# Block 0's second product: half of it by seven block products, and one load of k moved behind the turns of x

## The chip, the cores and the metric

One core of one Trainium2 chip. The metric is device time in microseconds (us) of one execution. Engines: TensorE (PE, with its weight loads PEld), VectorE (DVE), ScalarE (ACT), GpSimd (POOL) and SyncE (SP), which here only issues DMAs.

## The reference

Batch 8, 8 heads, 576 positions, head dimension 64. A linear attention with cosine and sine features is followed by a two-layer network whose activation is a quick gelu:

```python
def phi(x, c, s):
    r = np.maximum(x, 0.0)
    return np.concatenate([r * c, r * s], axis=-1)
q_p, k_p = phi(q, cos_w, sin_w), phi(k, cos_w, sin_w)
kv = np.einsum('bhsf,bhsd->bhfd', k_p, v)
z = np.sum(k_p, axis=2)
num = np.einsum('bhsf,bhfd->bhsd', q_p, kv)
den = np.einsum('bhsf,bhf->bhs', q_p, z)[..., None] + 1e-06
x = num / den                  # to (4608, 512)
h = x @ w_in                   # (4608, 2048)
g = h * (1.0 / (1.0 + np.exp(-1.702 * h)))
return g @ w_out               # (4608, 512)
```

## The kernel before

A block is the first 512 tokens of one batch; the last 64 tokens of each batch are gathered into one tail that is worked at the end. All matmuls take bf16 and accumulate in fp32. The order of the instructions on every engine is the order in which the code emits them (a manual schedule), so each engine is a queue that stops at its first unmet wait.

For each batch, VectorE or ScalarE makes the features of k (`trig`, line 161: two instructions, cosine and sine, for each of nine slices) and of q (`trig_q`, line 176, two for each of five chunks), and v is cast (`vcopy`, line 187). SP turns q's features with DMA transposes (`qturn_dma`, 217). A key/value product of 72 matmuls (`kv_next`, 794, line 237) is evacuated by VectorE (line 245). `num_mm` (304) makes numerator and denominator of one chunk of 128 tokens, `num_div` (315) divides on VectorE in three instructions (lines 321, 323, 325), and the chunk is turned into x's layout, by TensorE and ScalarE (`xturn_mm`, `xturn_evac`) for batch 1 or by a DMA on SP (`xturn_dma`, 351) from batch 2 on.

The first product (x by w_in) fills accumulators of the PSUM pool `pmm`, which has four banks taken in turn; ScalarE writes the gelu of each to g. The second product (g by w_out) has 16 steps of 128 (`fc`). In the blocks from 1 on it is done by seven block products instead of eight (`wino_mm`, 509): g and w_out are cut in two along the inner dimension, g along its tokens and w_out along its columns, VectorE makes four sums of blocks of g (`g_sums`, 466) and four of blocks of w_out (`w_sum_1`, `w_sums`, 441 to 451, made once), and seven products p1, p2, p6, p5, p7, p3, p4 go to three banks w, y and x. Between the products a bank is copied by ScalarE (`keep`, 528) or added to a kept copy by VectorE (`join`, 539). Batches 2 to 6 do the same to part of the first product in pairs of units (`mm1_pair`, 724, class `Unit`).

Block 0 is different: its second product is plain. `mm2` (416) makes, for each of four groups of 128 tokens, 16 matmuls 512 columns wide, and ScalarE writes the bank to the result tile `ty` (line 427). These 64 matmuls stand between the tail of the first product (`mm1_tail_first`) and `start_block(1)` (798), which begins block 1's first product: four accumulators, chunk by chunk, while x's chunks 2 and 3 are divided and turned. In between stand the key/value product of batch 1 and the chunks 0 to 2 of its x. On VectorE the features of k of batch 1, the sums of w_out and three of the five chunks of q stand beside it.

The loads of the batches go through SP's queue: q, k and v of batch 2 after batch 1's turns of q (lines 935, 936). In block 1, at `fc` 6, the features of batch 2's k are made, and then k and q of batch 3 are loaded, k first:

```python
if nb is not None and fc == f0 + 1:
    kv_operands(nb)
    if nb + 1 < B:
        load(kf, k, nb + 1, nc.sync)
        load_q(nb + 1, nc.sync)
```

Then come block 1's seven products, between which batch 2's x is made and turned by SP (`x_next`), v of batch 3 is loaded after the fourth turn, and ScalarE makes the features of batch 3's q. `mm1_pair` for batch 2 begins with the sums of x (line 635 on) and the features of batch 3's k on VectorE, among which the additions of the paired units stand (line 667).

Of the kernel before, what the change touches and what calls it, by code (L numbers as in the profile page):

```python
# [9 lines left out]
F32 = mybir.dt.float32  # L10
BF16 = mybir.dt.bfloat16
AF = mybir.ActivationFunctionType
MUL = mybir.AluOpType.mult
ADD = mybir.AluOpType.add
MAX = mybir.AluOpType.max
SUB = mybir.AluOpType.subtract
# [4 lines left out]
def kernel(  # L21
# [9 lines left out]
    nc = tc.nc  # L31
    B, H, S, D = q.shape
    d_model = H * D
    d_ff = moe_w_in.shape[1]
    KC = d_model // 128
    FC = d_ff // 128
    NS = S // 64
# [7 lines left out]
    ypool = ctx.enter_context(tc.tile_pool(name="ypool", bufs=4))  # L45
    small = ctx.enter_context(tc.tile_pool(name="small", bufs=3))
    pmm = ctx.enter_context(tc.tile_pool(name="pmm", bufs=4, space=PSUM))
# [76 lines left out]
    def load(t, src, b, eng=nc.gpsimd):  # L124
        eng.dma_start(out=t, in_=src_of(src, b))
# [50 lines left out]
    def trig_q(c, act=False):  # L176
        n = 128 if c < 4 else 64
        i = chunk(qf, c)
        for cs, w in enumerate((cosw, sinw)):
            o = qn[0:n, c, :, ts(cs, 64)]  # L180
            sc = w[0:n, NS + c:NS + c + 1]
            if act:
                nc.scalar.activation(o, i, AF.Relu, scale=sc)  # L183
            else:
                nc.vector.tensor_scalar(o, i, 0.0, sc, op0=MAX, op1=MUL)
# [31 lines left out]
    def qturn_dma(c):  # L217
        n = 128 if c < 4 else 64
        nc.sync.dma_start_transpose(out=qT[:, :, c * 128:c * 128 + n],
                                    in_=qn[0:n, c].rearrange("p h f -> p (h f)"))  # L220
# [108 lines left out]
    x = {}  # L329
# [43 lines left out]
    def mm1(b, fc):  # L373
        mm1_part(b, fc, 0, MT)
        gelu(fc)
# [9 lines left out]
    def mm1_tail_first(half):  # L385
        hps = pmm.tile([128, 8, 64], F32, name="mm")
        for f in range(8):
            for kc in range(KC):
                nc.tensor.matmul(hps[:, f], wcol(kc, half * 8 + f), xt[:, kc, 0:64],
                                 start=(kc == 0), stop=(kc == KC - 1))  # L390
        nc.scalar.activation(gt0[:, ts(half, 8)], hps, AF.Gelu_apprx_sigmoid)
# [7 lines left out]
                             hps[:, 64:B * 64].rearrange("p (b a t) -> p b a t", a=2, t=32),  # L399
                             AF.Gelu_apprx_sigmoid)  # L400

    yp = {}

    later = []
    out_j = out[0:S].rearrange("(p j) d -> j p d", j=NS)
# [1 line left out]
    def rows(b, t):  # L407

        if t == 4:
            return [(64 * u, 64, out_j[NS - 1] if b + u == 1 else out[(b + u) * S - 64:(b + u) * S])  # L410
                    for u in range(2)]
        if b == 0:
            return [(64 * u, 64, out_j[2 * t + u]) for u in range(2)]
        return [(0, 128, out[b * S:b * S + 512].rearrange("(p c) d -> c p d", c=4)[t])]

    def mm2(b, t, lo, hi, c0=0, c1=d_model):
        if lo == 0:
            yp[b, t, c0] = pmm.tile([128, d_model], F32, name="mm")
        for fc in range(lo, hi):
            w = gT[fc // 4][:, fc % 4, ts(t, 128)] if t < 4 else gt[:, fc, ts(b // 2, 128)]  # L420
            nc.tensor.matmul(yp[b, t, c0][:, c0:c1], w, w_out_sb[:, fc, c0:c1],  # L421
                             start=(fc == 0), stop=(fc == FC - 1))
        if hi == FC:
            if t % 2 == 0:
                st["y0"] = ypool.tile([128, 2, d_model], F32, name=f"ty{t // 2}", bufs=1)
            ysb = st["y0"][:, t % 2]
            nc.scalar.activation(ysb[:, c0:c1], yp[b, t, c0][:, c0:c1], AF.Identity)
            for p0, n, dst in rows(b, t):
                later.append((dst[:, c0:c1], ysb[p0:p0 + n, c0:c1]))

    HF = FC // 2
# [4 lines left out]
    sg = {n: sums[:, i].rearrange("p (f t) -> p f t", f=HF)  # L438
          for i, n in enumerate(("s1", "s2", "s3", "s4"))}

    def w_sum_1():
        nc.vector.tensor_tensor(wt["t1"], wq[0, 1], wq[0, 0], op=SUB)

    def w_sums(h):

        tt = nc.vector.tensor_tensor
        o = {n: wt[n][:, ts(h, 4)] for n in wt}
        w = {n: wq[n][:, ts(h, 4)] for n in wq}
        tt(o["t2"], w[1, 1], o["t1"], op=SUB)
        tt(o["t3"], w[1, 1], w[0, 1], op=SUB)  # L450
        tt(o["nt4"], w[1, 0], o["t2"], op=SUB)
# [256 lines left out]
    def pair_slot():  # L708
        pair_no[0] += 1
        return pair_slots[pair_no[0] % 7].rearrange("p (f t) -> p f t", f=2)  # L710

    def x_pair(b):
        t = xpool.tile([128, KC, MT], BF16, name="xT")
        xp[b] = {n: t[:, i].rearrange("p (k t) -> p k t", k=2) for i, n in enumerate(("t1", "t2", "t3", "nt4"))}
        for n in xp[b]:
            x_sum(b, n, xp[b])
# [81 lines left out]
    def start_block(b):  # L798

        for c in range(4):  # L800
            for fc in range(4):
                mm1_part(b, fc, c * 128, c * 128 + 128)
            if c == 0:
                num_mm(3)
                num_div(3)
                xturn_mm(2)
                xturn_evac(b, 2)
            if c == 1:
                num_mm(4)
                num_div(4)  # L810
                xturn_mm(3)
                xturn_evac(b, 3)
        for fc in range(4):
            gelu(fc)
        mm1(b, 4)
        xturn_dma(b, 4)
# [101 lines left out]
    load_wout(3)  # L918
    for n in ws_pair:
        win_sum(n, 0, ws_pair)  # L920
    for j in range(NS):
        trig(kr, kf, j)
    w_sum_1()
    for fc in range(8, FC):
        mm1(0, fc)
    mm1_tail_first(0)
    mm1_tail_first(1)
    for c in range(5):
        trig_q(c, act=(c > 2))
        qturn_dma(c)  # L930
    w_sums(0)
    vcopy(0, 2)
    vcopy(2, 4, act=True)
    w_sums(1)
    load_q(2, nc.sync)
    load_kv(2)
    for g in range(2):
        for t in range(4):
            mm2(0, t, 4 * g, 4 * g + 4)
    for t in range(4):  # L940
        mm2(0, t, 8, 12)
    kv_next()
    mm2(0, 0, 12, 16)
    x_open(1)
    num_mm(0)
    num_div(0)
    mm2(0, 1, 12, 14)
    num_mm(1)
    num_div(1)
    mm2(0, 1, 14, 16)  # L950
    xturn_mm(0)
    xturn_evac(1, 0)
    mm2(0, 2, 12, 16)
    xturn_mm(1)
    xturn_evac(1, 1)
    num_mm(2)
    num_div(2)
    mm2(0, 3, 12, 16)
    start_block(1)

    def kv_operands(b):
        for j in range(NS):
# [4 lines left out]
    def x_next(b, c):  # L967
        num_mm(c)
        num_div(c)
        xturn_dma(b, c)  # L970


    for b in range(1, B):
        nb = b + 1 if b + 1 < B else None
        if nb is None:
            break
        f0 = 5 if b == 1 else 0
        if b in PAIR:
            mm1_pair(b, nb)
        for fc in range(f0, FC) if b not in PAIR else ():  # L980
            if b == 1 and fc == f0:
                for c in range(5):
                    trig_q(c)
                    qturn_dma(c)
            if nb is not None and fc == f0 + 1:
                kv_operands(nb)

                if nb + 1 < B:
                    load(kf, k, nb + 1, nc.sync)
                    load_q(nb + 1, nc.sync)  # L990
            if fc == 8 and b == 1:
                vcopy()
            if fc == 12:
                g_sums(("s1", "s2"), 0)
            mm1(b, fc)
        if nb is not None:
            x_open(nb)
            if b == 1:
                kv_mm_next()
            g_sums(("s1", "s2"), 1)  # L1000
            if b == 1:
                kv_evac(0, 4)
                g_sums(("s3",), 0)
            at = ({2: [0], 3: [1], 4: [2], 6: [3], 8: [4]} if b == 1 else
                  {s: [p if nb < B - 1 else (0, 4, 1, 2, 3)[p]] for p, s in enumerate((0, 1, 3, 4, 6))})
            wino_open()
            for p in range(7):
                for c in range(2):
                    wino_mm(p, c)
                    s = 2 * p + c  # L1010
                    if c == 1:
                        wino_after(b, p)
                    for c2 in at.get(s, ()):
                        x_next(nb, c2)
                        if c2 == 3 and nb + 1 < B:
                            load(vf, v, nb + 1, nc.sync)

                    s0 = 4 if b > 2 else 8
                    if s0 <= s < s0 + 5 and nb + 1 < B:
                        trig_q(s - s0, act=True)  # L1020
                    if 8 <= s < 13 and nb + 1 < B:
                        qturn_dma(s - 8)
                    if s == 4 and b > 1:
                        for n in ("s3", "s4"):
                            g_sums((n,), 0)
                            g_sums((n,), 1)
                    if s == 2 and b == 1:
                        g_sums(("s3",), 1)
                    if s == 4 and b == 1:
                        g_sums(("s4",), 0)  # L1030
                    if s == 6 and b == 1:
                        g_sums(("s4",), 1)
            if nb in PAIR:
                x_pair(nb)
# [107 lines left out]
```

## Time and profile before

| what | value |
|---|---|
| median of three runs | 274.7 us (274.24 to 275.27) |
| the profiled execution | 274.66 us, its span 272.9 us |
| granted TensorE clock | 0.998 |
| 64 matmuls of block 0's second product, line 421 | 33.42 to 50.30, with other work between |
| key/value product of batch 1 / of batch 2 | starts at 43.88 / 65.49 |
| first matmul of block 1, line 365 | 50.13 |
| first paired block (batch 2) | from 80.13 |

The profile gives start, duration, engine, line, operation and tiles of each instruction, in us from the span's start. A bracket at the end of a row tells how long the engine was idle before it and what ended that. Instructions of one engine overlap: the next starts somewhat before the one before it has ended, so the distance of starts, not the duration, is the price of one in a series. A matmul's end is modelled, too. A DMA has its issue on its queue and a landing, which is a mark on a semaphore from each of 16 engines.

### The profile page before, as it was taken

How to read it: one execution, taken by the hardware profiler on the slowest of the kernel's cores; microseconds unless marked ns; L12 is line 12 of the kernel's file. 1: busy time of each engine (PE TensorE's matmuls, PEld its weight loads, DVE VectorE, ACT ScalarE, POOL GpSimd, SP SyncE). 2: the span in 40 equal slices, each digit the busy share in tenths (PEclk: the TensorE clock that was granted, in tenths of full speed). 3: DMA queues.
4: the chain of work that ended last, by engine and by line, in shares of the span. 5: the costliest groups of instructions: out<-in, count | busy, mean ns of one | idle time of the engine just before them, and what ended most of it. 6: DMA issues, size and time to landing. Idle time of an engine off the chain costs nothing.

```text
span 272.9 us, 7034 instructions
## 1 busy us (share of the span) xinstructions
PE 264.9 (97%) x2844; PEld 206.3 (76%) x2864; DVE 207.8 (76%) x487; ACT 174.7 (64%) x316; POOL 39.8 (15%) x66
## 2 busy tenths in 40 slices
PE   8899999999999999999999999999999999999995
PEld 2585645856986788778877887788778876999984
DVE  4947766689869799779988898789888995744741
ACT  6967632585289728983888487858684147677621
POOL 5691000000121012101110022001300173000010
PEclk9999999999999999999999999999999999999999
DMA  7999999999999979999999699999990654000343
GB/s 240 252 211 299 270 297 144 252 325 173 337 228 309 243 202 175 194 209 320 235 280 250 193 142 260 171 286 208 231 214 4 108 154 137 0 2 0 78 116 115
DMA packets 74031, 53.66 MB, mean 197 GB/s; under 512 B 53024, under 2 KB 63776, under 8 KB 74000
## 3 DMA queue, kind: packets, MB, share of 16 engines
q1 hardware_dynamic: 68032, 37.37, 61.6%
q0 software_dynamic: 5968, 15.86, 23.9%
q8 instruction: 22, 0.36, 0.6%
q14 instruction: 9, 0.07, 0.1%
HBM read 36.70 MB, written 9.44 MB: 169 GB/s over the span
## 4 chain that ended last, share of the span: by engine, by line
PE 88%; DVE 4%; ACT 3%; DMA 2%; issue 1%; SPq 0%; ACTq 0%
PE mm L520 28%; PE mm L658 15%; PE mm L365 13%; PE at L721 9%; PE mm L421 5%; PE at L520 4%; PE mm L396 4%; PE at L237 4%; PE at L310 3%; DMA kf<-in_k_dram 2%; ACT qn L183 2%; DVE xn L325 1%; DVE kr L169 1%; PE at L342 1%; PE mm L205 1%
## 5 line engine op out<-in xcount | busy, mean ns | idle before, releaser
L520 PEld LDWEIGHTS <-sums 128*128 128x128 bf16 x448 | 41.8, 98 | 6.0 <-DVE sums L477 1.1
L526 POOL DMA_DIRECT2D out_dram<-ysb x24 | 17.4, 725 | 180.5 <-DVE den L321 101.1
L520 PE MATMUL mm<-wsum,sums 128*128 128x256 bf16 x336 | 40.6, 273 | 0.0
L365 PE MATMUL mm<-xT,w_in 128*128 128x512 bf16 (+1 forms) x240 | 37.8, 304 | 1.1 <-issue 0.9
L520 PEld LDWEIGHTS <-g 128*128 128x128 bf16 x336 | 32.0, 98 | 4.6
L371 ACT ACTIVATE g<-mm 128x512 bf16<-128x512 f32 x42 | 24.1, 598 | 9.9 <-PE mm L365 9.9
L365 PEld LDWEIGHTS <-w_in 128*128 128x128 bf16 x248 | 21.3, 114 | 11.7
L721 PE MATMUL at<-xT,w_in 128*128 128x512 bf16 x110 | 27.8, 379 | 0.5
L325 DVE TENSOR_TENSOR xn<-at,inv 128x512 bf16<-128x512 f32 x39 | 27.0, 691 | 1.3
L520 PE MATMUL mm<-w_out_sb,g 128*128 128x256 bf16 x224 | 27.4, 273 | 0.0
L169 DVE TENSOR_SCALAR kr<-kf,cosw 128x256 bf16<-128x256 f32 x69 | 24.5, 355 | 3.6 <-DMA kf<-in_k_dram 3.6
L169 DVE TENSOR_SCALAR kr<-kf,sinw 128x256 bf16<-128x256 f32 x68 | 23.6, 348 | 0.0
L658 PE MATMUL mm<-xT,w_in 128*128 128x256 bf16 x152 | 22.0, 273 | 0.0
L658 PE MATMUL mm<-xT,gt 128*128 128x256 bf16 x160 | 21.6, 272 | 0.4 <-ACT gt L672 0.4
L183 ACT ACTIVATE qn<-qf,cosw 128x512 bf16<-128x512 f32 (+1 forms) x27 | 19.2, 711 | 3.6 <-DMA qf<-in_q_dram 2.6
L658 PEld LDWEIGHTS <-w_in 128*128 128x128 bf16 x168 | 18.6, 113 | 3.3
L658 PEld LDWEIGHTS <-gt 128*128 128x128 bf16 x160 | 17.6, 113 | 2.8 <-issue 0.5
L721 PEld LDWEIGHTS <-w_in 128*128 128x128 bf16 x120 | 13.5, 113 | 8.2
L183 ACT ACTIVATE qn<-qf,sinw 128x512 bf16<-128x512 f32 (+1 forms) x27 | 19.1, 708 | 0.0
L371 ACT ACTIVATE g<-at 128x512 bf16<-128x512 f32 x30 | 17.5, 597 | 2.0 <-PE at L721 1.3
L535 ACT ACTIVATE kept_p<-mm 128x512 f32<-128x512 f32 (+1 forms) x15 | 8.5, 565 | 16.0 <-PE mm L520 14.2
L535 ACT ACTIVATE kept_u<-mm 128x512 f32<-128x512 f32 (+1 forms) x8 | 4.3, 544 | 18.9 <-PE mm L520 18.9
(175 smaller groups left out, 467.7 us busy)
## 6 DMA issues: line engine op xcount, KB each, us to landing
kf<-in_k_dram SPq DMA_DIRECT2D x6, 1152.0 KB, 9.6
vf<-in_v_dram SPq DMA_DIRECT2D x6, 1152.0 KB, 6.6
qf<-in_q_dram SPq DMA_DIRECT2D x6, 1024.0 KB, 6.0
out_dram<-ysb POOLq DMA_DIRECT2D x24, 256.0 KB, 5.5
w_out_sb<-in_moe_w_out_dram POOLq DMA_DIRECT2D x4, 512.0 KB, 17.6
kf<-in_k_dram POOLq DMA_DIRECT2D x1, 1152.0 KB, 13.2
vf<-in_v_dram POOLq DMA_DIRECT2D x1, 1152.0 KB, 21.0
w_in<-in_moe_w_in_dram POOLq DMA_DIRECT2D x2, 512.0 KB, 10.1
```

What stands on the lines that cost most here:

```text
L169: eng.tensor_scalar(o, i, 0.0, w[:, j:j + 1], op0=MAX, op1=MUL)
L183: nc.scalar.activation(o, i, AF.Relu, scale=sc)
L237: nc.tensor.matmul(st["kv", i][:, hh, ds(col, n)], kr[r, j, i, :], rhs(r, i, j), start=(j == 0), stop=(j == NS - 1))
L325: nc.vector.tensor_tensor(xn, pv[:, :, :, 0:64], inv.unsqueeze(3).to_broadcast([128, 2, 4, 64]), op=MUL)
L365: nc.tensor.matmul(hp[fc][:, t0:t1], wcol(kc, fc), x[b][:, kc, t0:t1], start=(kc == 0), stop=(kc == KC - 1))
L371: nc.scalar.activation(gT[fc // 4][:, fc % 4], hp.pop(fc), AF.Gelu_apprx_sigmoid)
L421: nc.tensor.matmul(yp[b, t, c0][:, c0:c1], w, w_out_sb[:, fc, c0:c1], start=(fc == 0), stop=(fc == FC - 1))
L520: nc.tensor.matmul(bank[to][c], lhs, rhs, start=opens, stop=(fc == HF - 1), skip_group_check=True)
L526: eng.dma_start(out=dst[:, 2 * i + c0:2 * i + c1, ts(n, HD)], in_=t[:, c0:c1])
L535: nc.scalar.activation(o, i, AF.Identity)
L658: nc.tensor.matmul(to[:, j], lhs, rhs, start=(opens and j == 0 and k == 0), stop=(k == 1), skip_group_check=True)
L721: nc.tensor.matmul(hp[fc], wcol(kc, fc), x[b][:, kc], start=(kc == 0), stop=(kc == KC - 1))
```

## The change

Two things are changed. The inner steps 0 to 7 of block 0's second product are done by seven block products on half-size blocks, with an extra bank z; the steps 8 to 15 are then added by plain matmuls 256 wide into the four banks. The sums of g's blocks go to the tile `sums`, those of w_out there too (the t1 sum stays in `wsum`); two of k's nine slices go from VectorE to ScalarE, the last two chunks of q's features are emitted after the copy of p5, and the second half of the sums of w_out for later blocks is emitted after `start_block(1)`. Three of the four results are written by VectorE (with the kept copy added), one by ScalarE; they go to DRAM where they did before. And the load of k of batch 3 is emitted after the fourth turn of batch 2's x, ahead of the load of v.

```diff
-    def w_sum_1():
-        nc.vector.tensor_tensor(wt["t1"], wq[0, 1], wq[0, 0], op=SUB)
+    def w_sum_1(h):
+        nc.vector.tensor_tensor(wt["t1"][:, ts(h, 4)], wq[0, 1][:, ts(h, 4)], wq[0, 0][:, ts(h, 4)], op=SUB)
...
+    def g_sums_0():
+        tt = nc.vector.tensor_tensor
+        o = sums0
+        tt(o["s1"], g0(1, 0), g0(1, 1), op=ADD)
+        tt(o["s2"], o["s1"], g0(0, 0), op=SUB)
+        tt(o["s3"], g0(0, 0), g0(1, 0), op=SUB)
+        tt(o["s4"], g0(0, 1), o["s2"], op=SUB)
+
+    def w_sums_0():
+        tt = nc.vector.tensor_tensor
+        o = sums0
+        w_sum_1(0)
+        tt(o["t2"], w0(1, 1), o["t1"], op=SUB)
+        tt(o["t3"], w0(1, 1), w0(0, 1), op=SUB)
+        tt(o["nt4"], w0(1, 0), o["t2"], op=SUB)
+
+    def open_0():
+        for n in ("x", "w", "y", "z"):
+            t = pmm.tile([128, 2, HD], F32, name="mm")
+            bank[n] = [t[:, c] for c in range(2)]
+            bank[n, "all"] = t
+
+    def prod_0(p):
+        name, to, a, w = PRODUCTS[p]
+        for c in range(2):
+            for f in range(4):
+                lhs = sums0[a][:, f, ts(c, 128)] if isinstance(a, str) else g0(a[1], a[2])[:, f, ts(c, 128)]
+                rhs = sums0[w][:, f] if isinstance(w, str) else w0(*w)[:, f]
+                nc.tensor.matmul(bank[to][c], lhs, rhs, start=(name in OPENS and c == 0 and f == 0),
+                                 stop=(name in OPENS and f == 3), skip_group_check=True)
+
+    def plain_0(to, i, n, lo, hi, cs=range(2)):
+        for c in cs:
+            for fc in range(lo, hi):
+                nc.tensor.matmul(bank[to][c], gT[fc // 4][:, fc % 4, ts(2 * i + c, 128)], wq[1, n][:, fc - HF],
+                                 start=(to == "z" and c == 0 and fc == HF), stop=(fc == FC - 1), skip_group_check=True)
...
+    def out_0(to, i, n, with_=None):
+        o = y0[i][:, :, ts(n, HD)]
+        if with_ is None:
+            nc.scalar.activation(o, bank[to, "all"], AF.Identity)
+        else:
+            nc.vector.tensor_tensor(o, bank[to, "all"], with_, op=ADD)
...
-    for j in range(NS):
+    g_sums_0()
+    for j in range(NS - 2):
         trig(kr, kf, j)
-    w_sum_1()
+    w_sums_0()
+    w_sum_1(1)
     for fc in range(8, FC):
         mm1(0, fc)
+    trig(kr, kf, NS - 2, act=True)
     mm1_tail_first(0)
+    trig(kr, kf, NS - 1, act=True)
     mm1_tail_first(1)
-    for c in range(5):
-        trig_q(c, act=(c > 2))
+    open_0()
+    prod_0(0)
+    keep("p1", "x")
+    prod_0(1)
+    prod_0(2)
+    for c in range(3):
+        trig_q(c)
         qturn_dma(c)
+    keep("u2", "x")
+    prod_0(3)
+    keep("p5", "y")
+    for c in (3, 4):
+        trig_q(c, act=True)
+        qturn_dma(c)
+    prod_0(4)
+    nc.vector.tensor_tensor(kept0, bank["x", "all"], kept["p5"], op=ADD)
     w_sums(0)
     vcopy(0, 2)
     vcopy(2, 4, act=True)
-    w_sums(1)
     load_q(2, nc.sync)
     load_kv(2)
-    for g in range(2):
-        for t in range(4):
-            mm2(0, t, 4 * g, 4 * g + 4)
-    for t in range(4):
-        mm2(0, t, 8, 12)
+    prod_0(5)
+    prod_0(6)
+    for to, i, n in (("w", 0, 0), ("y", 0, 1), ("x", 1, 0), ("z", 1, 1)):
+        plain_0(to, i, n, 8, 12)
     kv_next()
-    mm2(0, 0, 12, 16)
+    plain_0("x", 1, 0, 12, 16)
+    out_0("x", 1, 0)
     x_open(1)
     num_mm(0)
     num_div(0)
-    mm2(0, 1, 12, 14)
+    plain_0("w", 0, 0, 12, 16, (0,))
     num_mm(1)
     num_div(1)
-    mm2(0, 1, 14, 16)
+    plain_0("w", 0, 0, 12, 16, (1,))
+    out_0("w", 0, 0, kept["p1"])
     xturn_mm(0)
     xturn_evac(1, 0)
-    mm2(0, 2, 12, 16)
+    plain_0("y", 0, 1, 12, 16)
     xturn_mm(1)
     xturn_evac(1, 1)
     num_mm(2)
     num_div(2)
-    mm2(0, 3, 12, 16)
+    out_0("y", 0, 1, kept["u2"])
+    plain_0("z", 1, 1, 12, 16)
+    out_0("z", 1, 1, kept0)
...
     start_block(1)
+    w_sums(1)
...
-                    load(kf, k, nb + 1, nc.sync)
                     load_q(nb + 1, nc.sync)
...
                             x_next(nb, c2)
+                        if c2 == 3 and b == 1:
+                            load(kf, k, nb + 1, nc.sync)
                         if c2 == 3 and nb + 1 < B:
                             load(vf, v, nb + 1, nc.sync)
```

More of the change, by code (lines that the diff above doesn't have):

```diff
@@ L400, in mm1_tails @@
                              AF.Gelu_apprx_sigmoid)
-    yp = {}
     later = []
@@ L414, in rows @@
         return [(0, 128, out[b * S:b * S + 512].rearrange("(p c) d -> c p d", c=4)[t])]
[L416 to L429, printed above, removed]
     HF = FC // 2
@@ L710, in pair_slot, with g0, w0 @@
         return pair_slots[pair_no[0] % 7].rearrange("p (f t) -> p f t", f=2)
+    sums_flat = sums.rearrange("p n e -> p (n e)")
+    sums0 = {n: sums_flat[:, ts(i, 1024)].rearrange("p (f t) -> p f t", f=4)
+             for i, n in enumerate(("s1", "s2", "s3", "s4", "t2", "t3", "nt4"))}
+    sums0["t1"] = wt["t1"][:, 0:4]
+    kept0 = pair_slots[0].rearrange("p (c d) -> p c d", c=2)
+    def g0(i, k):
+        return gT[k][:, :, ts(i, 256)]
+    def w0(k, n):
+        return wq[0, n][:, ts(k, 4)]
@@ new lines, in plain_0 @@
+    def plain_0(to, i, n, lo, hi, cs=range(2)):
[3 more added lines that the diff above has]
+                                 start=(to == "z" and c == 0 and fc == HF), stop=(fc == FC - 1), skip_group_check=True)
+    y0 = [ypool.tile([128, 2, d_model], F32, name=f"ty{i}", bufs=1) for i in range(2)]
+    def out_0(to, i, n, with_=None):
[4 more added lines that the diff above has]
+            nc.vector.tensor_tensor(o, bank[to, "all"], with_, op=ADD)
@@ L957 @@
     num_div(2)
-    mm2(0, 3, 12, 16)
+    out_0("y", 0, 1, kept["u2"])
+    plain_0("z", 1, 1, 12, 16)
+    out_0("z", 1, 1, kept0)
+    for t in range(4):
+        for p0, n, dst in rows(0, t):
+            later.append((dst, y0[t // 2][p0:p0 + n, t % 2]))
     start_block(1)
+    w_sums(1)
     def kv_operands(b):
```

## Prediction

> **What bounds the kernel now.** I read the busy shares first, then the chain of work that ended last, then the engines' timelines from 31 to 92 us, since the edits lie there. All sums are against the profiled execution, 274.66 us (span 272.9 and 1.8 around it); the median of the three runs is 274.7, so the two can be used for each other. A measurement of this kernel tells about 0.5% (1.37 us) from no change.
>
> ```profile
> PE 264.9 (97%) x2844; PEld 206.3 (76%) x2864; DVE 207.8 (76%) x487; ACT 174.7 (64%) x316; POOL 39.8 (15%) x66
> ...
> PE 88%; DVE 4%; ACT 3%; DMA 2%; issue 1%; SPq 0%; ACTq 0%
> ```
> TensorE is busy 97% and holds 88% of the chain: only less matmul time, or fewer of its few gaps, makes this shorter, and any wait put into its queue is paid in full. The windows of the edited stages say where gaps are:
>
> ```profile
> 33.42:43.88 10.46, 10.41 (x53) 4.62 (x52) 5.48 (x11) 4.33 (x6) 0.00 (x0) 1.00 1.11 239
> 43.88:50.13 6.25, 6.08 (x120) 3.78 (x121) 4.77 (x13) 2.79 (x5) 0.00 (x0) 1.00 1.07 152
> ...
> 80.13:95.12 14.99, 14.36 (x160) 10.80 (x162) 12.10 (x31) 13.77 (x27) 0.90 (x2) 1.00 1.06 290
> ```
> Columns: length, busy time of PE, PEld, DVE, ACT, POOL, then clock, DMA share and GB/s. The second product itself (33.42 on) has no gap to win; 0.63 us lie open from 80.13 on, in the first paired block.
>
> **Term 1, the products.** Removed: 64 matmuls 512 wide at line 421. Added: 7 products of 8 matmuls and 64 plain ones, 120 in all, 256 wide. Start to start the trace has 0.2158 us for the wide form and 0.1091 for the narrow one (line 520, the same shape). 64 x 0.2158 = 13.81; 120 x 0.1091 = 13.09; **-0.72**. At an exact half it would be 0.86; the narrow form's overhead takes the rest.
>
> **Term 2, waits inside the products.** p6, p7 and p4 write bank x only after it was copied (p1, u2) or added (kept0). ScalarE first has the last gelu (31.50), four trigs of k at 0.40 each and two tail gelus: it is free at 34.6, copies p1 until 35.13, and p6 is reached at 33.42 + 2 x 0.873 = 35.17: no wait. VectorE: the four block sums start at 26.31 and take 2.55 (rows of 0.61, 0.72 when dependent), 14 trigs 3.68, five half-size weight sums 3.1, six trigs of q 2.4: it reaches kept0 at 38.1, just as p7 is done, and ends at 38.78. p4 is reached at 38.66 and waits to 38.84: **+0.18**. The weights' groups 0 and 1 landed at 28.95 and 31.35, before use. If these covers fail by 0.4 each, the term is 0.6; at best it is 0.
>
> The key/value product follows, and its evacuation, which before started 0.15 late behind the second half of the weight sums (44.74 on, VectorE); these move away: **-0.15**. So PE reaches block 1's first matmul at 50.13 - 0.69 = 49.44.
>
> **Term 3, the banks of block 1.** Three of the four result banks now go out on VectorE (0.60 apart, 0.68 long, rows of line 545) instead of ScalarE (0.60). The two last stand in VectorE's queue behind the division of x chunk 2, whose product row is this:
>
> ```profile
> 49.91 0.69 DVE L325 TENSOR_TENSOR xn<-at,inv 128x512 bf16<-128x512 f32 x1
> ...
> 54.13 0.49 DVE L185 TENSOR_SCALAR qn<-qf,cosw 128x512 bf16<-128x512 f32 x1
> ...
> 59.35 0.35 DVE L169 TENSOR_SCALAR kr<-kf,cosw 128x256 bf16<-128x256 f32 x1 [1.18 <-DMA kf<-in_k_dram]
> ...
> 64.08 1.35 DVE L193 CAST vt<-vf 128x2304 bf16<-128x2304 f32 x1
> ```
> Shifted by -0.70 that row starts at 49.21; y goes out 49.81 to 50.49, z 50.42 to 51.10. Block 1's third and fourth accumulators take just these banks, and PE wants them at 49.88 and 50.10. The fourth starts at 51.15; before it started at 50.98. The lead of 0.69 has become a delay of 0.17: **+0.86**. Behind the waiting matmul stand the products of x chunk 3, and behind them VectorE's next divisions, so both run 0.17 late from here.
>
> **Term 4, the moved weight sums.** They now follow the last division, 3 x 0.605 = 1.81 us, before the ten trigs of q (54.13 above), the 18 of k and the cast of v. The 1.18 us that VectorE waited for k at 59.35 hide part; what is left is the path 54.22 + 1.81 + 3.98 + 4.73 + 1.35 = 66.09 (54.22: the last division's end less the overlap that the rows show), against 65.43 before. Block 2's key/value product started at 65.49, with no slack to the cast; now at 66.15: **+0.49** on top of the 0.17, PE 0.66 late. SP's five turns of q stay paced by their queue (55.48 to 66.36).
>
> **Term 5, q of batch 3 lands earlier.** These rows are of SP's queue, ScalarE and PE:
>
> ```profile
> 66.46 0.53 SPq L125 DMA_DIRECT2D kf<-in_k_dram  x1
> 67.05 0.49 SPq L128 DMA_DIRECT2D qf<-in_q_dram  x1
> ...
> 70.92 6.31 SPq L354 DMA_TRANSPOSE xT<-xn  x4
> 77.28 0.58 SPq L125 DMA_DIRECT2D vf<-in_v_dram  x1
> ```
> ```profile
> 76.44 0.72 ACT L183 ACTIVATE qn<-qf,cosw 128x512 bf16<-128x512 f32 x1 [0.99 <-DVE sums L479]
> ```
> ```profile
> 83.69 1.08 PE L658 MATMUL mm<-xT,gt 128*128 128x256 bf16 x8 [0.35 <-ACT gt L672]
> ```
> The page blames VectorE for ScalarE's 0.99, but q's last landing mark is at 76.37: q had k's 1.15 MB ahead of it in SP's queue. With k gone q lands near 73, ScalarE runs the ten trigs 0.99 earlier, and the copy that PE waits for at 83.69 is no longer late. PE could have issued at 83.16: **-0.53**. PE is then 0.13 late.
>
> **Term 6, k itself.** k is issued after the fourth turn of x. That turn waits for its chunk's division, so it is issued at 76.5 (76.01 before), and k at 77.8 instead of 66.46. In paired block 2 VectorE's first work after the sums of x is k:
>
> ```profile
> 82.14 0.35 DVE L169 TENSOR_SCALAR kr<-kf,cosw 128x256 bf16<-128x256 f32 x1
> ...
> 87.08 0.69 DVE L667 TENSOR_TENSOR kept_p<-gt,mm 128x512 f32<-128x512 f32 x1 [0.58 <-ACT g L371]
> ...
> 88.74 0.68 DVE L667 TENSOR_TENSOR gt<-gt,mm 128x512 f32<-128x512 f32 x1
> ```
> With it stand, in order, six trigs, an add, eight trigs, an add, four trigs and the add at 88.74: 18 x 0.263 + 2 x 0.605 + 0.68 = 6.62 us without idle time. PE's four matmuls into the bank that this add reads start at 89.47, 0.05 after it ends: no slack. If k lands at K, they start at K + 6.72; without a wait at 89.47 + 0.13 = 89.60. So k costs nothing up to K = 82.88 and its lateness beyond. Bounds of K: from below 79.5 (the turn's issue and 3.0, a landing of the next block's turns) + 3.0 (1.18 MB at the 397 to 399 GB/s of 81 to 83) + 0.4 (last bytes to last mark) = 82.9; from above 9.6, the median of k's landings in its tile's view, 87.4. The nearest rows are v in this very place: it landed 3.83 after the last turn (80.59 to 84.42), which with the next block's median turn of 3.7 gives 76.5 + 3.7 + 3.83 = 84.0; in later blocks 6.4 to 6.9 after its issue, 84.2 to 84.7, with transfers ahead that are absent here. I take **84.1**: 84.1 + 6.72 = 90.82, **+1.22**.
>
> [...]
>
> Behind k on SP's queue stand v, the last turn of x and five turns of q. v lands near 87.4, its cast comes at 90.8; the turns landed between 84.9 and 91.3 and are read from 96 on, which covers k's 3 us. Nothing later gives the time back: every later wait stands as before, only later.
>
> **Sum.** -0.72 + 0.18 - 0.15 + 0.86 + 0.49 - 0.53 + 1.22 = 1.35: 274.66 + 1.35 = **276.0 us**, 0.49% over before.
>
> **Rivals.**
> - *k in time.* The turns, freed of q and k ahead of them, let k's packets through at once, and K is at most 82.88: only the 0.13 stays, 274.8, not slower than before. For it: 397 GB/s is there. Against: no load of k or v with landing marks took under 6.4, and this asks for 5.1.
> - *VectorE not late.* If y and z go out in time, the lead of 0.69 lasts to block 2's key/value product; there k, landed at 59.33, binds the trigs as before, unless its load too comes 0.7 earlier. With k of batch 3 issued 0.66 earlier (K = 83.45) PE loses 0.7; with that in time as well it gains 0.53, and 1.2 if the lead lasted: 273.4 to 275.4, at the very edge 273.2. Against it: on VectorE the division stands first, by the order of the program.
> - *k far too late.* Mixed with v, written outputs and turns, k takes 8 to 9.6 after issue: from K = 85.8 VectorE's adds hold PE for 2.9 us and more: 277.7 to 279.3, clearly slower. For it: the loads of k in the paired blocks took 9.45 to 9.8 behind q. Against: here q is long done.
> - *The products do not pay.* p6, p7 and p4 each wait 0.4 for their copy: term 2 is 1.2 instead of 0.18: 277.0.
>
> **How the numbers follow.** Forecast 0.58 (275.2 to 277.2; half of it beyond +0.5%), k in time 0.15, VectorE not late 0.10 (half of it, its early end, counted as faster), k far too late 0.11, products do not pay 0.06. Slower by over 0.5%: 0.29 + 0.11 + 0.06 = 0.46; faster by over 0.5%: 0.05; within: 0.49. The range, 274.4 to 277.6, takes in the second case and leaves out most of the third and all of the fourth.
>
> **What would show it.** Term 1: 120 matmuls 0.109 apart from 33.4 on. Term 3: a gap of 0.6 and one of 0.4 in PE near 50, ended by VectorE's writes of y and z. Term 4: the key/value product at 66.1, released by the cast. Term 5: ScalarE's trigs of q right behind the copy of p5. Term 6: VectorE idle from 82 to 84 for k, then a PE gap of about 1.2 us before 91. If VectorE does not wait for k there, the sum is wrong by that much.

## The result, and the profile after

The kernel after takes **277.03 us** (median of 6 runs, 276.59 to 277.71) and the kernel before, beside it, 274.23 (6 runs, 273.96 to 275.27): ratio 1.0099, 95% interval 1.0076 to 1.0121, so about 2.8 us slower. The profiled execution of after took 276.59 us, its span 274.8. Against the profiled execution of before (274.66, 272.9) that is 1.93 more, where the sum said 1.35. The two profiled runs stand closer together than the medians: that of before is 0.43 over its median, that of after is the fastest of its six.

From the page of after, the busy shares and the chain that ended last:

```profile
PE 266.7 (97%) x2920; PEld 211.7 (77%) x2920; DVE 213.0 (78%) x495; ACT 176.1 (64%) x320; POOL 39.9 (15%) x66
...
PE 75%; DMA 12%; DVE 6%; POOL 3%; ACT 2%; issue 1%; SPq 0%; POOLq 0%; DVEq 0%
```
TensorE's busy share hides the change; the chain shows it. Of before's 88% TensorE keeps 75, and transfers take 12% in place of 2, so more of the end hangs on landings.

The windows of after (columns as in the prediction) for the same three stretches:

```profile
33.42:43.88 10.46, 10.44 (x126) 9.04 (x125) 8.04 (x15) 6.62 (x12) 0.00 (x0) 1.00 1.09 239
43.88:50.13 6.25, 5.66 (x120) 5.00 (x113) 4.09 (x11) 1.79 (x3) 0.00 (x0) 1.00 1.11 156
...
80.13:95.12 14.99, 14.01 (x108) 10.55 (x108) 11.19 (x31) 13.27 (x26) 1.61 (x3) 1.00 1.09 286
```
The products themselves are still without a gap. The second stretch had 0.17 us open and has 0.59; the third has 0.98 in place of 0.63.

TensorE's rows of after between 46 and 92 us that waited for another engine or for a transfer:

```profile
46.94 0.42 PE L310 MATMUL at<-kvs,qT 128*128 128x65 bf16 x8 [0.59 <-DMA qT<-qn]
51.17 0.41 PE L365 MATMUL mm<-xT,w_in 128*128 128x128 bf16 x4 [0.50 <-DVE ty L754]
51.77 0.38 PE L365 MATMUL mm<-xT,w_in 128*128 128x128 bf16 x4 [0.18 <-DVE ty L754]
66.72 1.26 PE L237 MATMUL at<-vt,kr 64*128 64x65 bf16 x72 [0.38 <-DVE vt L193]
91.19 0.60 PE L642 MATMUL mm<-xT,gt 128*128 128x256 bf16 x4 [0.98 <-DVE gt L651]
```
Four of the five were forecast, with their releasers. The first was not: numerator 1 waits for the turn of q's chunk 1, which landed at 45.38 before and lands at 46.89 here. And these are the rows of VectorE that the prediction shifted:

```profile
49.83 0.69 DVE L325 TENSOR_TENSOR xn<-at,inv 128x512 bf16<-128x512 f32 x1
...
65.32 1.34 DVE L193 CAST vt<-vf 128x2304 bf16<-128x2304 f32 x1
...
84.53 0.35 DVE L169 TENSOR_SCALAR kr<-kf,cosw 128x256 bf16<-128x256 f32 x1 [2.56 <-DMA kf<-in_k_dram]
```

| mark (us) | before | after | moved | forecast of the move |
|---|---|---|---|---|
| key/value product of batch 1 | 43.88 | 43.42 | -0.46 | -0.54 |
| numerator 3, in block 1's first product | 51.20 | 51.99 | +0.79 | +0.17 |
| key/value product of batch 2 | 65.49 | 66.72 | +1.23 | +0.66 |
| key/value product of batch 3 | 93.25 | 94.97 | +1.72 | +1.35 |

Behind the last mark after takes 0.13 longer than before. The profile of after starts its first work on the edited stages 0.1 later than that of before (33.52, 33.42).

### The profile page after: what moved, and what is told of

It reads as the page before. It is cut to its first block, busy times and chain, and to the rows that moved or that the text cites. A ratio compares the mean times of both kernels' runs of the same rounds, so it can differ in the third digit from the quotient of the medians.

```text
span 274.8 us, 7183 instructions
## 1 busy us (share of the span) xinstructions
PE 266.7 (97%) x2920; PEld 211.7 (77%) x2920; DVE 213.0 (78%) x495; ACT 176.1 (64%) x320; POOL 39.9 (15%) x66
## 4 chain that ended last, share of the span: by engine, by line
PE 75%; DMA 12%; DVE 6%; POOL 3%; ACT 2%; issue 1%; SPq 0%; POOLq 0%; DVEq 0%
PE mm L504 31%; PE mm L642 15%; PE at L765 9%; DMA vf<-in_v_dram 7%; PE at L504 4%; PE mm L396 4%; PE mm L365 4%; DMA qT<-qn 3%; PE at L310 3%; PE at L237 3%; DVE kr L169 2%; DMA kf<-in_k_dram 2%; DVE qn L185 1%; ACT qn L167 1%; POOL qn L169 1%; ACT kr L167 1%
## 5 line engine op out<-in xcount | busy, mean ns | idle before, releaser
L365 PE MATMUL mm<-xT,w_in 128*128 128x512 bf16 (+1 forms) x248 | 39.4, 307 | 0.7 <-DVE ty L754 0.7
L765 PE MATMUL at<-xT,w_in 128*128 128x512 bf16 x120 | 29.2, 379 | 0.0
L169 DVE TENSOR_SCALAR kr<-kf,cosw 128x256 bf16<-128x256 f32 x67 | 23.8, 355 | 4.9 <-DMA kf<-in_k_dram 4.9
L169 DVE TENSOR_SCALAR kr<-kf,sinw 128x256 bf16<-128x256 f32 x66 | 22.7, 344 | 0.0
L519 ACT ACTIVATE kept_p<-mm 128x512 f32<-128x512 f32 (+1 forms) x17 | 9.7, 569 | 16.5 <-PE mm L504 16.2
L519 ACT ACTIVATE kept_u<-mm 128x512 f32<-128x512 f32 (+1 forms) x9 | 5.0, 550 | 20.2 <-PE mm L504 19.1
```

Source lines behind the costliest of these rows:

```text
L169: eng.tensor_scalar(o, i, 0.0, w[:, j:j + 1], op0=MAX, op1=MUL)
L365: nc.tensor.matmul(hp[fc][:, t0:t1], wcol(kc, fc), x[b][:, kc, t0:t1], start=(kc == 0), stop=(kc == KC - 1))
L519: nc.scalar.activation(o, i, AF.Identity)
L765: nc.tensor.matmul(hp[fc], wcol(kc, fc), x[b][:, kc], start=(kc == 0), stop=(kc == KC - 1))
```

## The experiments

All runs at a glance: ratio to the kernel before beside them (its medians were 274.17 to 274.43), then from each trace the start of the fetch of instructions that is explained below, the landing of chunk 1's turn, the start of the key/value product of batch 2, and the stretch from there to that of batch 3. Each kernel has one trace.

| kernel | median us | ratio, 95% interval | fetch | turn lands | batch 2 | stretch |
|---|---|---|---|---|---|---|
| before | 274.23 | 1 | 45.69 | 45.38 | 65.49 | 27.76 |
| after | 277.03 | 1.0099 (1.0076 to 1.0121) | 44.77 | 46.89 | 66.72 | 28.25 |
| b1_k_behind | 276.78 | 1.0097 (1.0084 to 1.0110) | 46.15 | 45.05 | 65.44 | 30.42 |
| a1_k_first | 275.89 | 1.0070 (1.0051 to 1.0089) | 44.50 | 46.61 | 66.44 | 27.20 |
| a4_q_trigs_early | 276.90 | 1.0108 (1.0094 to 1.0123) | 44.52 | 46.64 | 66.47 | 28.16 |
| a3_sums_back | 276.30 | 1.0073 (1.0060 to 1.0085) | 44.67 | 46.78 | 66.28 | 28.41 |
| a5_kv_later | 276.25 | 1.0071 (1.0057 to 1.0085) | 45.24 | 47.13 | 66.49 | 28.53 |
| b5_kv_sooner | 274.17, one run | - | 45.52 | 45.15 | 65.55 | 27.20 |
| b2_q_then_k | 274.15 | 0.9998 (0.9985 to 1.0012) | 46.15 | 45.00 | 65.47 | 27.22 |
| c1_kv_later_k_swap | 275.97 | 1.0056 (1.0032 to 1.0080) | 45.52 | 47.38 | 66.70 | 27.16 |
| b6_halves | 274.51 | 1.0026 (0.9999 to 1.0053) | 45.45 | 45.13 | 65.47 | 27.28 |
| d1_all_mended | 275.07 | 1.0028 (1.0001 to 1.0054) | 45.15 | no mark | 65.60 | 28.31 |
| b7_quarters | 276.15 | 1.0051 (1.0032 to 1.0070) | 43.62 | 46.83 | 65.84 | 28.88 |
| a2_y_first | 276.30 | 1.0067 (1.0054 to 1.0080) | 44.16 | 46.29 | 66.07 | 28.22 |

**The two parts, each alone.** *b1_k_behind* is the kernel before with only the load of k moved:

```diff
-                    load(kf, k, nb + 1, nc.sync)
                     load_q(nb + 1, nc.sync)
...
+                        if c2 == 3 and b == 1:
+                            load(kf, k, nb + 1, nc.sync)
```


> The kernel before with one edit: k of batch 3 is loaded behind the fourth turn of batch 2's x, as in the changed kernel; block 0 is as before. Theory (k is late): k is issued near 77.2, lands near 83.4, VectorE idles for it after the sums of x, and PE's four matmuls into the bank that VectorE's third add reads start at 83.4 + 6.72 = 90.1 instead of 89.47; the gap before 83.69 closes, but that is hidden by the later wait. Batch 3's key/value product starts 0.65 later than 93.25, time +0.65 (ratio to before 1.002). Rival (the move of k is the gain and block 0 alone is the loss): the gap of 0.53 closes and VectorE is not late where it counts: -0.5, ratio 0.998.

*a1_k_first* is the kernel after with the same edit undone, so block 0's part alone.

> The changed kernel with one edit undone: k of batch 3 is loaded ahead of q again. Theory (k is late): PE's wait of 0.98 at 91.19 is gone, the gap near 83.7 comes back; batch 3's key/value product starts at 93.25 + 1.23 = 94.5 instead of 94.97, time 0.5 below the changed kernel (276.5), still about 0.8 percent over before. Rival 1 (only block 0 costs): no difference to the changed kernel, 277.0. Rival 2 (the move is a gain of 0.53): 277.5.

By medians block 0 alone costs 1.7 us, k's load alone 2.6, both together 2.8: they don't add. The theory of b1 had 0.65, and that of a1 had 276.5 with the gap near 83.7 back: in a1's trace that gap is absent, and batch 3's product starts at 93.64. Of a1's loss 0.95 stands at batch 2's mark; a gap of TensorE of 0.40 at 129.37, which no wait in the trace explains, comes on top. TensorE in b1, from 38 to 97 us, waits twice, both times for additions of VectorE that stand behind its features of k, and the first of those waits for k:

```profile
87.73 0.60 PE L658 MATMUL mm<-xT,w_in 128*128 128x256 bf16 x4 [1.84 <-DVE gt L667]
92.08 0.60 PE L658 MATMUL mm<-xT,gt 128*128 128x256 bf16 x4 [1.14 <-DVE gt L667]
```
```profile
85.42 0.35 DVE L169 TENSOR_SCALAR kr<-kf,cosw 128x256 bf16<-128x256 f32 x1 [4.43 <-DMA kf<-in_k_dram]
```
k landed at 85.39 there and at 84.50 in after. b1's theory had it issued near 77.2 and landed near 83.4. SP's rows of b1 show a part of the difference:

```profile
70.87 7.26 SPq L354 DMA_TRANSPOSE xT<-xn  x4
78.18 0.58 SPq L125 DMA_DIRECT2D kf<-in_k_dram  x1
```
The four turns hold SP for 7.26 us (6.31 before, 6.12 in after), and k is issued 2.41 behind the fourth. A fetch of instructions (explained below) starts at 75.61 in that trace and the turns stand still from 76.3 to 78.1; that it delays k here is argued from its place, not shown. In the six kernels with the late load (after, b1, a2, a3, a4, a5) the key/value product of batch 3 starts 10.47 or 10.48 us behind k's landing, whatever block 0 did: k's landing alone sets the start of batch 3, and block 0's delay is covered up to it. That is why the parts don't add: b1 is 1.28 us ahead of after at batch 2's mark (65.44, 66.72), but k lands 0.89 later there, and its stretch is 2.17 longer.

**Where block 0's part loses its time.** *a3_sums_back* puts the second half of the sums of w_out back to where it was.

```diff
     vcopy(2, 4, act=True)
+    w_sums(1)
...
     start_block(1)
-    w_sums(1)
```


> The changed kernel with one edit undone: the second half of the sums of w_out stands again behind the cast of batch 1's v, ahead of the evacuation of its key/value product. Theory (these 1.8 us hold batch 2's cast of v): the evacuation is 0.6 later, which the late turn of q hides; batch 2's features start at once after the last division, its key/value product at 66.28 instead of 66.72 (then bound by PE), time 276.6. Rival (VectorE's 1.8 us are covered by its wait for k of batch 2): no change at 66.72, and the later evacuation costs up to 0.6: 277.0 to 277.6.

The wait for the cast of v is gone (66.28 without a gap), as the theory has it; 0.47 us comes back as a wait for `kvs` at 46.00, and the later wait for k takes 1.14 where it took 0.98. The total moves to 276.30.

*a4_q_trigs_early* brings the features of q ahead of a sum, so that chunk 1's turn is issued sooner.

```diff
     w_sums_0()
-    w_sum_1(1)
...
     w_sums(0)
+    w_sum_1(1)
```


> The changed kernel with one edit: the second half of the first sum of w_out (0.6 us on VectorE) stands behind the features of q instead of ahead of them, so these start at 35.4, as before. Theory (the turn of q's chunk 1 is late because its features are): the turn lands near 45.5 instead of 46.89, PE's wait of 0.59 before 46.94 goes (0.97 in starts), and all behind it moves by that, batch 2's key/value product from 66.72 to 65.75, time 276.1. Rival (the turn lands when the queue lets it, whatever the features do): landing stays at 46.9, no gain, 277.0.

My theory of the late turn fell here: it was issued at 37.72, as early as in before (37.70), and still landed at 46.64. The issue isn't what makes it late.

*a2_y_first* copies y out ahead of division 2.

```diff
+    out_0("y", 0, 1, kept["u2"])
     num_mm(2)
     num_div(2)
-    out_0("y", 0, 1, kept["u2"])
```


> The kernel after with one edit: y is copied out ahead of numerator 2 and its division, not behind them. Theory (term 3 of the prediction, mis-sized there): the first product of block 1 waits 0.50 us at 51.17 for y's bank because VectorE's copy of y stands behind division 2, and 0.18 at 51.77 for z's; with y's copy 0.6 us sooner the first of these waits goes, z's stays or grows to at most 0.3: 0.4 us less than the kernel after, if nothing later takes it back. Rival: the wait only moves (division 2 is now later, and with it the turn of x's chunk 2), or the key/value product of batch 2 waits for the cast of v all the same (its gap at 66.72 grows from 0.38 to 0.8): the time of the kernel after.

```profile
51.11 0.38 PE L365 MATMUL mm<-xT,w_in 128*128 128x128 bf16 x4 [0.58 <-DVE ty L754]
66.07 1.26 PE L237 MATMUL at<-vt,kr 64*128 64x65 bf16 x72 [0.39 <-DVE vt L193]
90.50 0.60 PE L642 MATMUL mm<-xT,gt 128*128 128x256 bf16 x4 [0.94 <-DVE gt L651]
```
The two waits of 0.50 and 0.18 have become one of 0.58: it moved from y's bank to z's, as the rival said. That numerator 1 doesn't wait in this trace is the turn's doing (it landed at 46.29), not the edit's. So the 0.7 us by which its median lies under that of after, taken in another group of runs, isn't shown to be this edit's.

**Why the turn is late.** The trace records the transfers of a queue whose kind it calls `instruction`. One such packet of 16 KB stands close to the turns of q in every trace. The view of the DMA queues over 43 to 48 us, in 40 slices of 0.125 us, shows what all queues moved, first in the kernel before:

```profile
GB/s 45 8 16 223 289 263 293 285 295 117 201 293 295 269 287 283 295 279 287 289 291 363 242 250 248 92 33 18 0 0 0 2 8 8 10 8 10 12 258 289
```
and in the kernel after:

```profile
GB/s 49 16 53 266 283 269 291 287 293 141 174 291 287 287 386 268 270 244 16 0 0 0 2 8 10 8 10 10 35 274 293 293 263 291 289 287 285 295 293 257
```
The slice with the highest rate (363, 386) holds the instruction packet, at 45.69 and 44.77. Within 0.7 us behind its start the turns stop almost wholly, and they run at full rate again 2.0 and 1.8 us behind it. In before chunk 1's turn had just landed; in after it was not yet complete, and sat through the stop. Over the whole execution that queue brings 22 packets in before and 23 in after, where TensorE has 5708 and 5840 matmuls and weight loads (259 and 254 to a packet). From 36 to 108 us the trace of after puts 166 to 320 of TensorE's instructions (matmuls and weight loads) between two such packets, 243 on average. That the packets hold TensorE's instructions was my estimate from these counts; the trace doesn't say whose they are. If they do, the change, which makes 120 matmuls in place of 64, each with its weight load, moves their fetches: the one near the turns stood at 45.69 before and stands at 44.77 after.

The first test of this, *a5_kv_later*, is a3 with block 0's end in another order:

```diff
-    kv_next()
     plain_0("x", 1, 0, 12, 16)
     out_0("x", 1, 0)
+    kv_next()
+    plain_0("w", 0, 0, 12, 16)
     x_open(1)
     num_mm(0)
     num_div(0)
-    plain_0("w", 0, 0, 12, 16, (0,))
     num_mm(1)
     num_div(1)
-    plain_0("w", 0, 0, 12, 16, (1,))
...
+    out_0("y", 0, 1, kept["u2"])
+    plain_0("z", 1, 1, 12, 16)
     xturn_mm(1)
     xturn_evac(1, 1)
     num_mm(2)
     num_div(2)
-    out_0("y", 0, 1, kept["u2"])
-    plain_0("z", 1, 1, 12, 16)
```


> The kernel after with w_sums(1) back at its old place, and with the key/value product of batch 1 put behind eight more plain products (0.87 us), and the products of the numerators 0 and 1 put behind all of w's products, so that nothing waits for the later product; y and z are closed and copied out ahead of numerator 2. Theory: the turn of chunk 1 of q lands late because the 16 KB of instructions that TensorE fetches stall its packets; TensorE reaches that place in its program as it ends the key/value product, so with that product 0.87 us later the fetch comes at about 45.5 and not at 44.8, behind the turn's last packet; the turn lands at about 45.5 (46.9 in the kernel after, 46.6 without this move), the wait of 0.59 us at numerator 1 is gone, the key/value product of batch 2 starts at about 65.5 (66.3 without it), and the time is about 275.5 (276.3 without it). Rival: the turn is late for what stands in the DMA queues at that time, which this doesn't change: it lands at 46.6 to 46.9 again and the time stays at 276.2 or more.

The fetch moved by 0.57 of the 0.87, and still met the turn's end: 47.13. z's copy, now behind division 2 alone, held TensorE for 1.25 us at 51.95. The turn's landing and the time were both missed.

*b5_kv_sooner* is the mirror image in the kernel before.

```diff
-    for t in range(4):
+    for t in range(3):
         mm2(0, t, 8, 12)
     kv_next()
+    mm2(0, 3, 8, 12)
```


> The kernel before with one edit: the key/value product of batch 1 goes ahead of the last four 512-wide products of inner blocks 8 to 11 (0.86 us of TensorE). Theory: the instruction fetch that comes at 45.7 in the kernel before, behind the last packet of chunk 1's turn, comes at about 44.8 and stalls that turn, which lands at about 46.7 and not at 45.4; no queue, load or turn is moved by the edit. Numerator 1 starts at 46.7, so little of it is waited for (about 0.2 us). Rival: the landing depends on what the DMA queues hold, and stays at 45.4.

The fetch moved by 0.17, not by 0.9, and the turn had landed: it says nothing on the cause of the late turn. *b6_halves* changes only the number of instructions:

```diff
+            if b == 0 and t < 4 and fc < 8:
+                for h in range(2):
+                    nc.tensor.matmul(yp[b, t, c0][:, ts(h, 256)], w, w_out_sb[:, fc, ts(h, 256)],
+                                     start=(fc == 0 and h == 0), stop=False, skip_group_check=True)
+                continue
```


> The kernel before, with the 32 products of inner blocks 0 to 7 of block 0 (512 columns each) each made as two of 256 columns: the same work, loads, turns and order, but 64 more instructions on TensorE ahead of the key/value product of batch 1 (32 products and 32 weight loads). Theory: it is the number of TensorE's instructions that sets when the next 16 KB of them are fetched, and that fetch stops the turns of q; here it comes 0.4 to 1 us sooner than in the kernel before (45.5 to 46.2 in the traces of it), so at 44.8 to 45.3, falls on chunk 1's turn, and that lands at 46.8 to 47.0 and not at 45.0 to 45.4. The time changes little (0.1 to 0.4 us more: numerator 1 starts at 46.75 and would wait a little). Rival: the seven block products' own traffic or order makes the turn late: here it lands at 45.0 to 45.4, and the time is the same within 0.1 us.

Here too it stopped short: fetch at 45.45, turn landed at 45.13, time within 0.5%. *b7_quarters* goes further the same way (four of 128 columns each for `fc < 4`).

> The kernel before, with the 16 products of inner blocks 0 to 3 of block 0 made as four of 128 columns each and the 16 of inner blocks 4 to 7 as two of 256: the same work, loads, turns and order, but 128 more instructions on TensorE ahead of the key/value product of batch 1 (b6_halves had 64 more, its fetch came at 45.45, only 0.3 us behind the landing of chunk 1's turn at 45.13). Theory: the fetch comes with the count of instructions, so at 44.0 to 44.7; all turns stop from some 0.4 us behind it until 1.65 to 2.05 us behind it (as in the other traces), and chunk 1's turn, which is on its way until 45.0 to 45.4 in every trace with the products of the kernel before, lands at 46.0 to 46.9. Numerator 1 at 46.75 may wait by 0.2 us, no more: 274.2 to 274.7. Rival: the products of the kernel after make the turn late, not the fetch: it lands at 45.0 to 45.4 though the fetch comes at 44.0 to 44.7.

```profile
GB/s 55 21 23 244 412 245 272 274 180 18 14 0 0 0 6 8 8 10 10 8 135 106 199 291 291 271 283 291 291 293 285 291 291 265 289 291 289 287 262 236
```
This separates the two. The loads, the turns and the order are those of the kernel before, the products too; only there are more of them. The fetch came at 43.62 (the slice of 412; 45.69 in before), the stop lasts from 44.1 to 45.5, and chunk 1's turn landed at 46.83. So the stop goes with the fetch, and the number of TensorE's instructions moves both. In all 14 traces the turns of q ran again 1.7 to 2.1 us behind the start of that fetch. By what means a fetch stops them no run shows.

Two limits stand beside this. The stop begins 0 to 0.8 us behind the fetch, and where it begins depends on the turns as well: in seven kernels (after, a1 to a5, c1) it comes when their queue has moved about 2600 packets from 36 us on, though the fetch starts anywhere from 44.16 to 45.52. So in these kernels a fetch 1.4 us later or sooner met the same turn. And the count places the fetch only roughly: in the 14 traces it comes behind some 970 to 1080 of TensorE's matmuls and weight loads (995 in before, 1077 in after).

I had not expected its 1.7 us of loss. Numerator 1 did not wait for the turn, since the extra instructions had put it at 47.10 already:

```profile
47.10 0.41 PE L310 MATMUL at<-kvs,qT 128*128 128x65 bf16 x8
```
At batch 2's mark the loss is 0.35 (65.84 against 65.49); the rest is in ScalarE's and TensorE's rows:

```profile
77.91 0.72 ACT L183 ACTIVATE qn<-qf,cosw 128x512 bf16<-128x512 f32 x1 [2.12 <-DMA qf<-in_q_dram]
```
```profile
85.16 1.08 PE L664 MATMUL mm<-xT,gt 128*128 128x256 bf16 x8 [1.48 <-ACT gt L678]
```
q of batch 3 landed at 77.84 and not at 76.4, and the wait of 0.35 that before has in this place is 1.48. What made q late there I haven't tested.

**Repairs.** *b2_q_then_k* swaps the two loads in the kernel before.

```diff
-                    load(kf, k, nb + 1, nc.sync)
                     load_q(nb + 1, nc.sync)
+                    load(kf, k, nb + 1, nc.sync)
```


> The kernel before with one edit: at the old place of both loads, q is loaded ahead of k. Theory (term 5 of the prediction): q lands some 4 us earlier, ScalarE starts q's rotary turns right behind keep p5 (at 75.5, not behind 76.7), the gap of 0.36 us ahead of 83.69 closes, and k still lands ahead of its first use at 82.1: 273.7 to 273.9 against 274.2 of before. Rival: ScalarE's work there is limited by something else, or k now comes too late: 274.2 or more.

The gap ahead of 83.69 is gone, but no time with it. b5 suggests why: it has the loads of before in their order, and its trace has no gap either:

```profile
75.94 0.72 ACT L183 ACTIVATE qn<-qf,cosw 128x512 bf16<-128x512 f32 x1 [0.44 <-DMA qf<-in_q_dram]
```
With q here 0.5 sooner than in the profiled run of before (76.44), ScalarE is in time. The same holds for b6 (75.94). So the gap is in the profiled execution of before, which is 0.43 us over its median, and not in every execution with this order of loads; how often it comes isn't shown.

*c1_kv_later_k_swap* is a5 with k loaded at its old place, behind q.

> The kernel a5_kv_later with, in addition, the load of k put back at its old place, but behind the load of q. If the two causes are apart and add: 1.1 us less than a5_kv_later for the wait for k (what a1_k_first gained), and 0.3 less for ScalarE's gap at 83.7: about 274.0, level with or just under the kernel before (274.2). Rival: k's wait was only hiding other late work (the cast of v, the turns of x), and the time stays above 275.

The 274.0 was missed, and the time stays above 275 as the rival says. The wait for k is gone (stretch 27.16), but runs scatter from 274.77 to 277.31, and the waits at 47.43 (0.35, the turn) and 52.17 (1.21, z's bank) stay. *d1_all_mended* takes c1 and covers these (`part(c, fcs)` issues block 1's products of chunk c for these fc):

```diff
+    plain_0("y", 0, 1, 12, 16, (0,))
     num_mm(1)
...
+    plain_0("y", 0, 1, 12, 16, (1,))
+    out_0("y", 0, 1, kept["u2"])
+    plain_0("z", 1, 1, 12, 16, (0,))
     xturn_mm(0)
     xturn_evac(1, 0)
+    plain_0("z", 1, 1, 12, 16, (1,))
...
+        part(0, (0, 1, 2))
+        num_mm(3)
+        num_div(3)
+        part(1, (0, 1, 2))
+        xturn_mm(2)
+        xturn_evac(b, 2)
+        part(0, (3,))
+        part(1, (3,))
```


> The kernel c1_kv_later_k_swap, with the order of TensorE around the end of block 0 spread so that its late partners are covered: half of y's products stand between numerators 0 and 1, half of z's ahead of the turn of x's chunk 0, w and y are copied out behind division 1, and the first product of block 1 leaves its fourth bank (z's) until both first chunks' other three are done. If the losses of block 0 are waits for the late turn and for the banks of y and z, as the traces of after and of a5_kv_later say (0.59 + 0.50 + 0.18 in the one, 0.32 + 1.25 in the other), 0.6 to 1.0 us goes and the time is about 275.1 by c1's median (275.97), its fastest runs at 273.9 to 274.2, where the kernel before has its own. Rival: VectorE, which copies w, y and z out and divides one after the other from 45.7 to 52.0, is the limit of that stretch, and the time stays at 275.6 or more.

It came out at 275.07, as the theory said. TensorE's waits for the turn and for y's and z's banks are gone, and the key/value product of batch 2 starts at 65.60, level with before. In its profiled run others came up, TensorE's rows at 80.73 and 82.05:

```profile
80.73 1.07 PE L642 MATMUL mm<-xT,w_in 128*128 128x256 bf16 x8 [0.33 <-DMA xT<-xn]
82.05 1.89 PE L765 MATMUL at<-xT,w_in 128*128 128x512 bf16 x8 [0.26 <-DMA xT<-xn]
```
The turns of batch 2's x are late there, with a fetch at 75.99 among them; that this fetch made them late is argued from its place, not shown. d1's fastest run, 274.19, reaches the median of before. No version beat the kernel before.

## Why the prediction was right, and where not

The first two of these rows of after are p3 and p4 (term 2), the third is ScalarE's first step of q (term 5):

```profile
37.91 1.04 PE L738 MATMUL mm<-w_out_sb,sums 128*128 128x256 bf16 x8
38.96 1.03 PE L738 MATMUL mm<-sums,g 128*128 128x256 bf16 x8
```
```profile
76.64 0.71 ACT L183 ACTIVATE qn<-qf,cosw 128x512 bf16<-128x512 f32 x1
```

- **Term 1, products**: right. The key/value product of batch 1 starts 0.46 sooner, forecast 0.54, less the 0.1 of the start. **Term 2**: the wait for kept0 is 0.18, as forecast: p3 and p4 start 1.05 apart, the products before them 0.87 to 0.88.
- **The step that failed** stands at the end of term 2: "So PE reaches block 1's first matmul at 50.13 - 0.69 = 49.44". It took the turn of q's chunk 1 as landed; the turn landed 1.51 later than before, and block 1 began at 50.06, 0.62 over the forecast. The sum has no term for that: its rows hold neither that turn's landing nor the instruction packets.
- **Term 3, banks**: right in kind. VectorE copies y and z out behind division 2 (49.83, 0.62 over the forecast 49.21, by the turn), and TensorE waits 0.50 and 0.18 for them (0.6 and 0.4 in the signs that the prediction names).
- **Term 4, moved sums**: right. The cast of v releases the key/value product of batch 2, 66.72 against the forecast 66.15: the 0.57 is the turn's 0.62 again. a3 shows the cast's part.
- **Term 5, q sooner**: the mechanism was right: ScalarE starts q at 76.64, directly behind the copy of p5, without a wait. Its 0.53 was read from one execution; b2 shows no gain from q's earlier landing where medians are compared. Before's profiled run holds that gap, which is a part of why the medians differ by 2.8 and the profiled runs by 1.9; the rest I can't assign.
- **Term 6, k**: right. K was 84.50 for 84.1, and K + 6.72 = 91.22 for TensorE's matmul at 91.19. Its wait was 0.98 for a forecast of 1.22, since TensorE came later by itself.

The terms were added up as if each stayed when another grew. They don't: with k late, TensorE starts batch 3 at K + 10.47, and block 0's delay is free until then. The 1.9 in the profiled pair is k's landing, not a sum; block 0's delay costs by way of k's issue, which stands behind batch 2's turns of x on SP (1.24 to 1.28 us behind the fourth's in five of the six kernels, 2.41 in b1).

That the time came out inside the range is in part luck. The sum gave block 0 (terms 1 to 4) 0.66 and the moved load (terms 5 and 6) 0.69; measured alone by medians they cost 1.7 and 2.6, and only because the one covers the other is the whole 2.8 and not 4.3.

## What to carry to other kernels

Splitting matmuls, or replacing them by more and narrower ones, moved a fetch of instructions here (from 45.69 in before to 43.62 in b7 and 44.77 in after), and the DMA turns in flight stood still behind it until 1.7 to 2.1 us after its start; a turn with less than two microseconds to spare belongs in the sum with a bound of its own. Where a chain passes a landing, add up what moves the landing, and take the larger of the branches, not their sum. And a gap of a third of a microsecond in one profiled run should be looked for in a second trace before it is counted as a gain.

## What the runs showed of the hardware

- A fetch of 16 KB of instructions (1.30 us for its one packet in before, 1.07 in after) went with a stop of the turns for 1.1 to 1.7 us in the 14 traces; moved by instruction count alone from 45.69 to 43.62, it took the stop with it, from 46.2 to 44.1.
- The place of the same fetch varies between programs that are equal up to there: 44.16 in a2 and 44.77 in after, 45.69 in before and 46.15 in b1 and b2. In before's program this decided which turn sat through the stop: chunk 2's (landing 47.89) in before, chunk 3's (48.58) in b1, where chunk 2's had landed at 45.95. In after's and a2's it was chunk 1's both times.
- A load of k (1.18 MB) took 6.1 to 6.4 us from issue to landing behind the turns of x in five kernels, and 7.2 in b1.
